# Four PSUM banks for the transposes of an attention kernel, and pauses that hold DMA issues back

## The chip, the cores and the metric

The kernel runs on one core of one Trainium2 chip. The metric is the device time of one execution in microseconds (us). The engines have these names in the profile: PE is the matmul engine (PEld its weight loads), DVE the vector engine, ACT the scalar engine, POOL the general engine, and SP the engine that here only issues DMAs (SPq is its queue).

## The reference

Attention over q, k, v of shape 4 batches x 8 heads x 576 rows x 64, with a threshold, then a Fourier mixing with an MLP, then a gated convolution:

```python
scores = q @ k.T / sqrt(64)
attn = exp(where(scores >= max(scores) - tau, scores, -1e9) - max(scores))
x = (attn / (sum(attn) + 1e-9)) @ v                  # heads side by side: 4 x 576 x 512
u = x + real(fft(fft(x, axis=seq), axis=features))
un = (u - mean(u)) / sqrt(var(u) + 1e-6)
y = u + relu(un @ w_ch1) @ w_ch2                     # 512 -> 2048 -> 512
out = (sigmoid(causal_conv5(y)) * (y @ w_val)) @ w_out
```

## The kernel before, in words

**Tiles.** Two heads make a pair, so there are 16 pairs, four for each batch. A pair has 9 tiles of 128 score rows by 576 keys: four of its first head, four of its second, and one that holds the last 64 rows of both. `g_tile(g)` describes the life of tile g (0 to 143), one step per `yield`:

- PE makes the scores `s` (L641) in one of two double banks of PSUM;
- DVE takes the negated row maximum `neg` (L706), ACT the exponential `e` (L712), DVE the thresholded product `p` with its row sum `su` (L723). After `p` the double bank of `s` is free for the scores of the tile after next;
- the reciprocal of `su` is taken for two tiles at once (L656, L658), and POOL scales `p` by it (L731);
- PE transposes `p` in four blocks into one bank `t` (L739), and ACT copies the bank to `m` (L756).

`g_tail` transposes the last 64 columns of each row tile (L668, L672), `g_pv` multiplies by v (L421) in ten matmuls for each part of a pair, `g_fold` and `g_mirror` fold the output with its mirror image by way of DRAM, and `g_fft` makes the Fourier transform of a batch (L540 and L553). The MLP's first chunk is `g_h` (L1201) and `g_c` (L1237), the mean for its variance is a matmul at L1113, and its other four chunks are L1047 and L1063.

**PSUM.** There are eight banks: four for `s`, two in `ps_t` for `t`, and two in `ps_f`, named `f`, for all other results (tails, v product, Fourier transform, means). Both pools are used in turn, so a new tile waits for the release of the one before the last of its own pool.

**What sets the order.** The kernel is written out by a planner at build time, `Loom`. Each generator asks for an engine, a cost in ns and a rank, or for a condition: `"after"` (marks of other generators), `"when"` (a test), `"delay"` (a time). `Loom.step` always takes the request that can start first by its own clock, and the code that follows the `yield` then emits the instructions. Each engine later runs what was emitted for it in exactly that order. So a rule or a cost of the planner changes the order of all five engines, and no instruction's own work. A request with `"room"` needs a bank of `ps_f`: `Loom.start` holds it until the tile before the last was freed.

Before the change, `"delay"` only moves the time from which the next engine request may start:

```python
elif kind == "delay":
    t.ready += args[0]
```

When the generator goes on with something that is not an engine request, such as a DMA on SP, the pause has no effect: the DMA is emitted at once. Three pauses are of that kind: the one ahead of `g_mirror` (L457 to L459), which reads back from DRAM (L440) what L453 has just stored there; 4000 ns ahead of the return of a conversion buffer (L916); and 200 ns ahead of the weight loads of `g_give`. Where a condition follows (`"when"` in `g_convert`), it is tested at once and buffers are taken at once, and only the engine request behind it keeps the pause.

**Weights.** The MLP's weights come as 64-bit numbers and are converted in pieces (`g_convert`: DVE L251, L252, L255 to L257, ACT L253, L254, POOL L261). The first pieces are stored to DRAM (`e_h`, `e_l`, SP L912) and loaded back (SP L872) once the attention's buffers are free; later ones are converted in place. Six `raw` and `cv` buffers carry this work.

Of the kernel before, what the change touches and what calls it, by code (L numbers as in the profile page):

```python
# [11 lines left out]
F32 = mybir.dt.float32  # L12
# [64 lines left out]
class Loom:  # L77
# [33 lines left out]
    def settle(self, t):  # L111
        while t.want is not None:
            kind, *args = t.want
            if kind == "after" and all(k in self.done for k in args):
                t.ready = max([t.ready] + [self.done[k] for k in args])
            elif kind == "delay":
                t.ready += args[0]
            elif kind == "when" and args[0]():
                t.ready = max(t.ready, self.clock)
            else:  # L120
                return
            t.want = next(t.gen, None)
            if t.want is None:
                self.tasks.remove(t)
# [16 lines left out]
    def start(self, t):  # L141
        e, ns, rank, *how = t.want
        s = max(self.now[e], t.ready)
        room = next((x for x in how if x.startswith("room")), None)
        if room:
            k = room, self.put.get(room, 0) - 2
            if k[1] >= 0:
                if k not in self.done:
                    return None
                s = max(s, self.done[k])  # L150
        return s

    def cost(self, t, s):
# [27 lines left out]

    def step(self, until=None):
        picks = [x for x in (self.pick(e) for e in self.now) if x]
        if not picks:
            return False
        s, t = min(picks, key=lambda x: x[0])
        if until is not None and s > until:
            return False
        e, ns, rank, *how = t.want
        ns = self.cost(t, s)  # L190
        if e == "PE":
            self.shape, self.last = how[0], t
        if "port" in how:
            self.port[e] = s + ns - 50.0
        self.now[e] = s + ns - self.OVER[e]
        self.clock = s
        self.end = s + ns + self.SIGNAL[e]
        t.ready = self.end
        self.pull(t)
        self.wake()  # L200
        return True
# [88 lines left out]
def attention_fft(tc, right, ps_f, a, u_d, dram, conv_w, loom):  # L290
    nc = tc.nc
    PE, DVE, ACT, POOL, SP = nc.tensor, nc.vector, nc.scalar, nc.gpsimd, nc.sync
    right1 = ExitStack()
    with ExitStack() as right2, ExitStack() as right2b, ExitStack() as right3, ExitStack() as right4, ExitStack() as scores, ExitStack() as turned:
        def pool(stack, name, bufs, side="right", **kw):
            return stack.enter_context(tc.tile_pool(name=name, bufs=bufs, side=side, **kw))
# [13 lines left out]
        ps_t = pool(turned, "ps_t", 2, space=PSUM)  # L310
# [73 lines left out]
        def fill_tile():  # L384
            return ps_f.tile([128, 512], F32, tag="f", name="f"), loom.room()
# [9 lines left out]
        def pt_tile(p, c):  # L395
            if (p, c) not in pt:
                pt[p, c] = (pt0_p, pt1_p)[c].tile([128, 2, 4, 256] if c == 0 else [128, 4, 640], F32, tag=f"m{c}", name=f"m{c}")
            return pt[p, c]

        def g_pv(p, c):  # L400
# [29 lines left out]
            if c == 1:  # L430
                loom.add(g_fold(p))
# [3 lines left out]
        def g_mirror(b):  # L435
            if b:
                yield "after", ("spent", b - 1)
            for i in range(2):
                m = mirror[b, i] = fft_p.tile([128, S], F32, tag=f"mirror{i}", name="mirror")
                SP.dma_start(out=m, in_=rev_d[b][i * 128:(i + 1) * 128])  # L440
            loom.mark("mirror", b, after=8000.0)

        def g_fold(p):
            b, j = p // NP, PAIRS[p % NP]
            yield "after", ("x", p, 0), ("x", p, 1), *([("folded", p - 1)] if p else [])
            x = xt.pop(p)
# [4 lines left out]
            if j >= 2:  # L451
                r = 1 + 128 * (3 - j)
                SP.dma_start(out=rev[r:r + 128], in_=x)  # L453
                if j == 2:
                    SP.dma_start(out=rev[0:1], in_=x[127:128])
                loom.mark("folded", p)
                if p % NP == 1:  # L457
                    yield "delay", 6000.0
                    loom.add(g_mirror(b))  # L459
                return  # L460
            SP.dma_start(out=xs[j * 128:(j + 1) * 128], in_=x)
# [5 lines left out]
            t = [tmp_p.tile([128, KE], F32, tag="xf", name="xf") for _ in range(2)]  # L467
# [214 lines left out]
        def g_tile(g):  # L682
            p, h, i = tiles[g]
            u, j = divmod(g, 2)
            c = 0 if i < 2 else 1
# [27 lines left out]
            if h != 1:  # L713
                n = p * 5 + i - PBUFS
                if n >= 0:
                    yield "after", ("tailed", *divmod(n, 5))
                    q, r = divmod(n, 5)
# [12 lines left out]
            v = p_view(g)  # L730
            POOL.tensor_scalar(out=v, in0=v, scalar1=ssum[u][:, j:j + 1], scalar2=1.0, op0=ALU.mult, op1=ALU.mult)  # L731
            loom.mark("n", g)
            yield "after", *([("t", g - 1)] if g else [("n", 0)]), *([("mc", g - 2)] if g > 1 else []), *([("pv", p - 2, c)] if p > 1 else [])
            yield "PE", 437.0, 0.5, "full"
            m = pt_tile(p, c)
            f = ps_t.tile([128, 4, 128], F32, tag="t", name="t")
            pv = v[:, TAIL if h == 1 else 0:]
            for t in range(4):
                PE.matmul(out=f[:, t, :], lhsT=pv[:, t * 128:(t + 1) * 128], rhs=ident, is_transpose=True, start=(t == 0), stop=(t == 3))  # L739
# [13 lines left out]
            else:  # L753
                x = h * 320 + (i - 2) * 128
                o, fv = m[:, :, x:x + 128], f
            ACT.activation(o, fv, AF.Copy)  # L756
            loom.mark("mc", g)

        idle = e_p.tile([128, 2, HALF], F32, tag="e", name="idle")[:, 0, 0:128]
        DVE.memset(idle, 0.0)  # L760
        f = ps_t.tile([128, 4, 128], F32, tag="t", name="idle")
# [20 lines left out]
        loom.end = 8500.0  # L782
        loom.mark("kq", 0)
        loom.add(g_tile(0))

        def g_late():
# [834 lines left out]
```

## Time and profile before

| | |
|---|---|
| median of 3 runs | 874.63 us (873.76 to 875.32) |
| the profiled execution | 873.72 us |
| its span, first to last instruction | 871.9 us |
| around the span | 1.82 us |
| busy share: PE, DVE, ACT, POOL | 95%, 64%, 48%, 44% |
| mean granted PE clock | 0.992 of full speed |

The attention takes the first 340 us, with the Fourier transform and the first weight conversions between its tiles. The MLP and the gate fill the rest. The profile gives, for each engine, its busy time, its idle time, and for an idle stretch the instruction that ended it (its releaser). A wait is put down to the engine whose signal came last.

### The profile page before, as it was taken

The page shows a single profiled execution, that of the slowest core. Times are in us where ns is not written, and L with a number is a line of the kernel's source. Part 1 is how long each engine was busy: PE and PEld are TensorE (multiplying, and loading weights), DVE is VectorE, ACT ScalarE, POOL GpSimd, SP SyncE. Part 2 cuts the span into 40 slices and gives each one's busy share as a digit, 9 for nine tenths or more (in the row PEclk, how much of TensorE's full clock was granted, in tenths as well). Part 3 has the DMA queues.
Part 4 walks back from the last instruction along what each step waited for, and adds up shares of the span by engine and source line. Part 5 has one row for each costly group of instructions (what it writes and reads, how often), then busy time and mean ns, then how long its engine had stood idle before and what let it go on. Part 6 is the DMA issues. An engine that isn't in the chain of part 4 may idle for free.

```text
span 871.9 us, 13881 instructions
## 1 busy us (share of the span) xinstructions
PE 830.0 (95%) x4886; PEld 653.7 (75%) x4886; DVE 556.8 (64%) x1212; ACT 421.0 (48%) x855; POOL 386.3 (44%) x450
## 2 busy tenths in 40 slices
PE   6999989989999997999999999999999999999998
PEld 4555556656656655788889999987888788898996
DVE  6999898888889985879846742223213646428740
ACT  3878777777758754664535332141123131134431
POOL 3466874597678564666443431013010210076421
PEclk9999999999999999999999999999999999999999
DMA  7369465536654338989316523004000320432111
GB/s 209 79 197 236 120 151 152 166 114 207 202 172 124 123 111 284 349 285 337 126 50 239 169 81 90 1 1 133 1 1 0 103 103 0 166 143 91 61 49 61
DMA packets 62733, 115.27 MB, mean 132 GB/s; under 512 B 14530, under 2 KB 21698, under 8 KB 62664
## 3 DMA queue, kind: packets, MB, share of 16 engines
q1 hardware_dynamic: 55128, 90.53, 32.5%
q0 software_dynamic: 7104, 23.57, 8.9%
q8 instruction: 39, 0.64, 0.3%
q10 hardware_dynamic: 432, 0.30, 0.2%
q14 instruction: 30, 0.25, 0.1%
HBM read 82.90 MB, written 31.47 MB: 131 GB/s over the span
## 4 chain that ended last, share of the span: by engine, by line
PE 65%; DVE 12%; issue 9%; ACT 6%; POOL 4%; DMA 3%; SPq 0%; DVEq 0%; ACTq 0%; POOLq 0%
PE c L1063 14%; PE h L1047 14%; PE f L421 6%; PE s L641 6%; PE v L1434 5%; PE o L1452 5%; PE c L1237 4%; PE h L1201 4%; PE t L739 4%; DVE neg L706 4%; DVE p L723 3%; ACT e L712 2%; POOL p L731 2%; ACT m L756 2%; PE f L540 1%
## 5 line engine op out<-in xcount | busy, mean ns | idle before, releaser
L731 POOL TENSOR_SCALAR p<-p,su 128x576 f32<-128x576 f32 x144 | 111.8, 786 | 96.7 <-DVE su L658 78.5
L1051 DVE SCALAR_TENSOR_TENSOR hl<-h,hh 128x384 fp32r<-128x384 f32 (+1 forms) x64 | 39.9, 624 | 150.4 <-ACT hh L1050 146.7
L1050 ACT ACTIVATE hh<-h 128x384 fp32r<-128x384 f32 (+1 forms) x64 | 34.8, 544 | 208.4 <-PE h L1047 202.3
L712 ACT ACTIVATE e<-s,neg 128x576 f32<-128x576 f32 x144 | 104.8, 742 | 55.2 <-DVE neg L706 41.5
L723 DVE SCALAR_TENSOR_TENSOR p<-s,thr,e 128x576 f32<-128x576 f32 x144 | 114.3, 816 | 12.9 <-ACT e L712 4.1
L641 PE MATMUL s<-kt,qt 64*128 64x288 f32 (+1 forms) x640 | 102.2, 453 | 13.5 <-DVE p L723 9.5
L706 DVE TENSOR_REDUCE neg<-s 128x1 f32<-128x576 f32 x144 | 103.9, 749 | 17.4 <-PE s L641 16.6
L739 PE MATMUL t<-ident,p 128*128 128x128 f32 x576 | 90.3, 286 | 13.6 <-ACT m L756 7.2
L739 PEld LDWEIGHTS t<-ident,p 128*128 128x128 f32 x576 | 63.7, 143 | 44.7 <-POOL p L731 23.1
L1063 PE MATMUL c<-hl,w1h 128*128 128x384 f32 (+1 forms) x256 | 92.8, 363 | 0.5 <-DVE hl L1051 0.5
L1063 PE MATMUL c<-hh,w1h 128*128 128x384 f32 (+1 forms) x256 | 92.6, 362 | 0.0
L1063 PE MATMUL c<-hh,w1l 128*128 128x384 f32 (+1 forms) x256 | 92.6, 362 | 0.0
L641 PEld LDWEIGHTS s<-kt,qt 64*128 64x128 f32 (+1 forms) x640 | 47.5, 181 | 54.6 <-issue 25.6
L756 ACT ACTIVATE m<-t 128x512 f32<-128x512 f32 x144 | 83.2, 599 | 4.8 <-PE t L739 4.2
L421 PE MATMUL f<-m,v 128*64 128x320 f32 (+1 forms) x512 | 72.5, 421 | 0.0
L1047 PE MATMUL h<-unh,w0h 128*128 128x384 f32 (+1 forms) x256 | 62.6, 364 | 1.2 <-ACT unh L1028 1.1
L1047 PE MATMUL h<-unl,w0h 128*128 128x384 f32 (+1 forms) x256 | 62.4, 363 | 0.3
L1047 PE MATMUL h<-unh,w0l 128*128 128x384 f32 (+1 forms) x256 | 61.6, 362 | 0.0
L421 PEld LDWEIGHTS f<-m,v 128*64 128x64 f32 x512 | 34.4, 140 | 28.1 <-issue 9.2
L1072 POOL TENSOR_TENSOR res<-ht,res 128x512 f32<-128x512 f32 (+1 forms) x20 | 23.0, 1185 | 68.7 <-DVE ht L1071 68.7
L1063 PEld LDWEIGHTS c<-hl,w1h 128*128 128x128 f32 x256 | 48.1, 188 | 6.3 <-DVE hl L1051 1.3
L1047 PEld LDWEIGHTS h<-unh,w0h 128*128 128x128 f32 x256 | 46.7, 188 | 7.5 <-ACT unh L1028 2.5
(259 smaller groups left out, 1662.9 us busy)
## 6 DMA issues: line engine op xcount, KB each, us to landing
raw<-in_moe_w_ch POOLq DMA_DIRECT2D x32, 512.0 KB, 5.6
qt<-in_q SPq DMA_DIRECT2D x30, 288.0 KB, 5.1
kt<-in_k SPq DMA_DIRECT2D x15, 432.0 KB, 3.9
ypad<-y_d SPq DMA_DIRECT2D x16, 288.0 KB, 4.1
out<-os SPq DMA_DIRECT2D x18, 256.0 KB, 2.0
v<-in_v SPq DMA_DIRECT2D x16, 256.0 KB, 2.7
e_h<-cx SPq DMA_DIRECT2D x16, 256.0 KB, 3.7
e_l<-ct SPq DMA_DIRECT2D x16, 256.0 KB, 2.3
```

What stands on the lines that cost most here:

```text
L421: PE.matmul(out=f[h * 64:h * 64 + 64, 0:n], lhsT=w, rhs=r, start=(t == 0), stop=(t == 4))
L641: PE.matmul(out=s[o, c, 0:HALF], lhsT=qt[w, hh, q], rhs=kt[w, 2 if h == 2 and hh else hh], start=True, stop=True)
L706: DVE.tensor_reduce(out=neg[u][:, j, 0:1], in_=sc[g][:, :, 0:HALF], axis=AX.XY, op=ALU.max, negate=True)
L712: ACT.activation(e, sc[g][:, :, 0:HALF], AF.Exp, bias=neg[u][:, j, 0:1], scale=1.0)
L723: DVE.scalar_tensor_tensor(out=p_view(g).rearrange("p (a b) -> p a b", a=2), in0=sc.pop(g)[:, :, 0:HALF], scalar=thr[u][:, j:j + 1], in1=e ...
L731: POOL.tensor_scalar(out=v, in0=v, scalar1=ssum[u][:, j:j + 1], scalar2=1.0, op0=ALU.mult, op1=ALU.mult)
L739: PE.matmul(out=f[:, t, :], lhsT=pv[:, t * 128:(t + 1) * 128], rhs=ident, is_transpose=True, start=(t == 0), stop=(t == 3))
L756: ACT.activation(o, fv, AF.Copy)
L1047: PE.matmul(out=f[:, 0:n], lhsT=ww[:, k * 128:(k + 1) * 128], rhs=x[:, k, 0:n], start=(i == 0), stop=(i == 3 * KB - 1))
L1063: PE.matmul(out=ch[c][o][:, 0:n], lhsT=ww[:, o * 128:(o + 1) * 128], rhs=x, start=(at_ == 0 and i == 0), stop=(at_ == FB - 1 and i == 2))
L1434: PE.matmul(out=f[:, 0:HALF], lhsT=w[:, k, o * 128:(o + 1) * 128], rhs=x[:, k, s], start=(i == 0), stop=(i == 3 * KB - 1))
L1452: PE.matmul(out=f, lhsT=x[:, k, d], rhs=w[:, k], start=(i == 0), stop=(i == 3 * KB - 1))
```

## The change

Three things change, all in the planner and its requests.

1. `"delay"` becomes a request of its own, `"until"`, that the planner's clock must reach before the generator goes on. Whatever follows, a DMA issue or the return of a buffer too, is emitted only then.
2. The transpose asks for `"room_t"` or `"room"`: the planner looks at the bank of `ps_t` and the bank of `ps_f` that would be next, and takes `ps_t` if it is free by then, else the one that is free first. The wait for mark `("mc", g - 2)`, the copy of the tile before the last, is gone; the copy now frees the bank that the tile took.
3. The pause ahead of the mirror's load is 8000 ns in place of 6000.

```diff
             elif kind == "delay":
-                t.ready += args[0]
+                t.want = "until", max(t.ready, self.clock) + args[0]
+                continue
+            elif kind == "until" and self.clock >= args[0]:
+                t.ready = max(t.ready, args[0])
...
-        room = next((x for x in how if x.startswith("room")), None)
-        if room:
-            k = room, self.put.get(room, 0) - 2
-            if k[1] >= 0:
-                if k not in self.done:
-                    return None
-                s = max(s, self.done[k])
+        rooms = [(x, self.put.get(x, 0) - 2) for x in how if x.startswith("room")]
+        if rooms:
+            free = [(self.done[k] if k[1] >= 0 else 0.0, k[0]) for k in rooms if k[1] < 0 or k in self.done]
+            if not free:
+                return None
+            when = min(free)[0]
+            t.place = next(x for w, x in free if w <= max(s, when))
+            s = max(s, when)
...
                 if p % NP == 1:
-                    yield "delay", 6000.0
+                    yield "delay", 8000.0
                     loom.add(g_mirror(b))
...
-            yield "after", *([("t", g - 1)] if g else [("n", 0)]), *([("mc", g - 2)] if g > 1 else []), *([("pv", p - 2, c)] if p > 1 else [])
-            yield "PE", 437.0, 0.5, "full"
+            yield "after", *([("t", g - 1)] if g else [("n", 0)]), *([("pv", p - 2, c)] if p > 1 else [])
+            yield "PE", 437.0, 0.5, "full", "room_t", "room"
             m = pt_tile(p, c)
-            f = ps_t.tile([128, 4, 128], F32, tag="t", name="t")
+            if loom.place == "room":
+                f, room = fill_tile()
+                f = f.rearrange("k (t q) -> k t q", t=4)
+            else:
+                f, room = ps_t.tile([128, 4, 128], F32, tag="t", name="t"), loom.room("room_t")
...
             ACT.activation(o, fv, AF.Copy)
+            loom.free(room)
             loom.mark("mc", g)
```

`step` also gains the lines that move the clock on to the next pause's end when no engine request starts before it.

The lines of the changed file are numbered higher: 641 becomes 651, 739 becomes 753, 421 becomes 431, 553 becomes 563, 1201 becomes 1216, 440 becomes 450, 872 becomes 887, 912 becomes 927. The order of the instructions changes on every engine. 132 of the 144 transposes still go to `ps_t`, 12 to `ps_f`. Three places follow.

PE in the middle of the attention, before: two score tiles (x4: two matmuls for each, four for the last tile of a pair; the trace shows each of them as two records), then the transposes of three tiles in one go (x12: four blocks each).

```order
L421 MATMUL f<-th_320_200,vt_196 64x320 x2
L641 MATMUL s<-kt,qt 128x288 x4
L739 MATMUL t<-ident,p 128x128 x12
L672 MATMUL f<-ident,p 64x64 x2
L641 MATMUL s<-kt,qt 128x288 x4
L739 MATMUL t<-ident,p 128x128 x4
```

The same piece of the program in the changed kernel (the end of the same v product, 64x320, stands in it).

```order
L651 MATMUL s<-kt,qt 128x288 x4
L431 MATMUL f<-m_1026,v_195 64x320 x2
L431 MATMUL f<-th_320_200,vt_196 64x320 x2
L753 MATMUL t<-ident,p 128x128 x8
L651 MATMUL s<-kt,qt 128x288 x4
L682 MATMUL f<-ident,p 64x64 x2
L431 MATMUL f<-m_1167,v_193 64x256 x6
L753 MATMUL t<-ident,p 128x128 x8
```

Two transposes at a time, and other work of PE behind them. Rows of x12 stand in the order before at five places, and at none in the changed order.

PE between the last score tiles and the MLP's first matmul, before: nine transposes follow the last scores, the last six of them here, with stage-2 matmuls of the third batch (L553) between; then the MLP's `h`, with the three last v products still to come behind it.

```order
L553 MATMUL f<-csl,aeh 128x290 x2
L739 MATMUL t<-ident,p 128x128 x4
L553 MATMUL f<-csl,aeh 128x290
L668 MATMUL f<-ident,p 128x128 x2
L739 MATMUL t<-ident,p 128x128 x8
L553 MATMUL f<-ssh,boh 128x290 x3
L739 MATMUL t<-ident,p 128x128 x8
L668 MATMUL f<-ident,p 128x128 x2
L739 MATMUL t<-ident,p 128x128 x4
L553 MATMUL f<-ssh,bol 128x290 x3
L553 MATMUL f<-ssl,boh 128x290 x3
L1201 MATMUL h<-unh,w0h_4203 128x512 x4
```

The same place now: six transposes follow the last scores, the last two of them here, and the tail and all three v products stand ahead of `h`.

```order
L563 MATMUL f<-ssl,boh 128x290 x2
L753 MATMUL t<-ident,p 128x128 x4
L678 MATMUL f<-ident,p 128x128 x2
L753 MATMUL t<-ident,p 128x128 x4
L682 MATMUL f<-ident,p 64x64 x2
L431 MATMUL f<-m_3898,v_193 64x320 x8
L431 MATMUL f<-th_320_198,vt_194 64x320 x2
L431 MATMUL f<-m_4099,v_195 64x256 x8
L431 MATMUL f<-th_256_199,vt_196 64x256 x2
L431 MATMUL f<-m_4228,v_195 64x320 x8
L431 MATMUL f<-th_320_200,vt_196 64x320 x2
L1216 MATMUL h<-unh,w0h_4202 128x512 x4
```

Two thirds of `h` 0 stood ahead of the v products before, none of it now. Between the v products and the variance's mean matmul (L1113) the order before has the rest of `h` 0, `h` 1, `c` 0, `h` 2 and three quarters of `c` 1 (the number is that of a block of 128 hidden units); the changed order has `h` 0, a third of `h` 1, 18 stage-2 matmuls of the third batch, `c` 0 and the rest of `h` 1. The fourth batch's first stage (L540) follows directly now; before, the rest of `c` 1 and a third of `h` 3 stood between. In DVE's queue the reciprocal for the last two tiles has two conversion instructions (L251, L252) ahead of it behind the last `p`, where there was one (L251).

SP's queue before the first load of converted weights, before: the mirror's load directly behind the store that it reads (xr_3861), and two stores of converted weights.

```order
L453 DMA xr_3861<-xt 128x576
L440 DMA mirror<-xr_3861 128x576 x2
L912 DMA e_h<-cx 128x512
L912 DMA e_l<-ct 128x512
L872 DMA w0h_4203<-e_h 128x512
```

The same place now: four stores of converted weights stand between the store (xr_3827) and its mirror's load.

```order
L463 DMA xr_3827<-xt 128x576
L927 DMA e_h<-cx 128x512
L927 DMA e_l<-ct 128x512
L927 DMA e_h<-cx 128x512
L927 DMA e_l<-ct 128x512
L450 DMA mirror<-xr_3827 128x576 x2
L887 DMA w0h_4202<-e_h 128x512
```

## Rows read from the trace of the kernel before

**Rows 1.** The page: the span, and the engines' busy time.
```profile
span 871.9 us, 13881 instructions
...
PE 830.0 (95%) x4886; PEld 653.7 (75%) x4886; DVE 556.8 (64%) x1212; ACT 421.0 (48%) x855; POOL 386.3 (44%) x450
```

**Rows 2.** Windows: length, busy time by engine (PE, PEld, DVE, ACT, POOL), clock, DMA.
```profile
20.00:326.00 306.00, 285.16 (x2089) 179.41 (x2093) 272.12 (x659) 226.43 (x492) 206.87 (x262) 0.98 0.53 153
340.00:450.00 110.00, 108.25 (x535) 86.93 (x534) 80.85 (x129) 56.03 (x106) 58.09 (x66) 0.99 0.71 244
450.00:760.00 310.00, 307.97 (x1529) 275.60 (x1529) 132.00 (x241) 84.75 (x148) 60.42 (x55) 1.00 0.23 76
```

**Rows 3.** Waits of PE: total us, times, longest.
```profile
PE s L641 <- DVE p L723: 9.5, 15, 2.1
PE t L739 <- ACT m L756: 7.2, 16, 0.8
PE t L739 <- POOL p L731: 5.4, 11, 0.8
PE h L1201 <- DMA w0h<-e_h: 4.3, 1, 4.3
```

**Rows 4.** Timeline of PE, 176 to 196 us: start, length, instructions, idle before.
```profile
178.27 1.09 PE L739 MATMUL t<-ident,p 128*128 128x128 f32 x8
180.10 0.63 PE L739 MATMUL t<-ident,p 128*128 128x128 f32 x4 [0.74 <-ACT m L756]
180.66 0.76 PE L641 MATMUL s<-kt,qt 64*128 64x288 f32 x4
...
189.00 1.24 PE L641 MATMUL s<-kt,qt 64*128 64x288 f32 x8
```

**Rows 5.** Timeline of PE, 296 to 350 us.
```profile
314.89 2.44 PE L641 MATMUL s<-kt,qt 64*128 64x288 f32 x8 [1.45 <-DVE p L723]
...
326.39 0.66 PE L739 MATMUL t<-ident,p 128*128 128x128 f32 x4
326.80 0.38 PE L553 MATMUL f<-csh,aeh 97*128 97x290 f32 x1
```

**Rows 6.** The chain that ended last: a stretch of stage-2 matmuls.
```profile
308.19 3.08 PE f L553 x23
```

**Rows 7.** Timeline of PE, 338 to 400 us.
```profile
338.75 1.82 PE L1201 MATMUL h<-unh,w0h 128*128 128x512 f32 x4 [4.27 <-DMA w0h<-e_h]
...
342.21 0.45 PE L672 MATMUL f<-ident,p 128*64 128x64 f32 x4
...
350.13 1.19 PE L1201 MATMUL h<-unl,w0h 128*128 128x512 f32 x4
...
353.89 0.39 PE L1237 MATMUL c<-hh,w1h 128*128 128x512 f32 x1
...
356.61 1.07 PE L1201 MATMUL h<-unh,w0h 128*128 128x512 f32 x4
...
362.66 0.50 PE L1113 MATMUL mean<-cs,ones 128*128 128x512 f32 x1 [0.89 <-DVE cs L1162]
...
364.62 0.40 PE L540 MATMUL f<-cdh,xeh 128*97 128x258 f32 x2
```

**Rows 8.** SP's queue: its waits at L440, and the first weight load's issue.
```profile
SPq L440 <- DMA xr<-xt: 11.9, 4, 5.3
...
334.04 0.49 SPq L872 DMA_DIRECT2D w0h<-e_h  x1
```

**Rows 9.** Timeline of POOL: the last two scalings of p, the fold's last step.
```profile
330.05 1.57 POOL L731 TENSOR_SCALAR p<-p,su 128x576 f32<-128x576 f32 x2 [3.73 <-DVE su L658]
...
361.37 0.70 POOL L485 TENSOR_TENSOR xel<-xf,xeh 128x289 fp32r<-128x289 f32 x1 [0.56 <-ACT xeh L483]
```

**Rows 10.** Windows around two long waits of PE; the clock is behind POOL's time.
```profile
314.00:320.00 6.00, 5.09 (x28) 2.59 (x30) 5.17 (x15) 2.69 (x6) 4.05 (x6) 0.72 0.55 180
338.00:344.00 6.00, 5.25 (x24) 3.40 (x26) 2.58 (x3) 0.22 (x1) 3.48 (x4) 0.72 1.00 356
```

More of the change, by code (lines that the diff above doesn't have):

```diff
@@ L183, in step @@
         picks = [x for x in (self.pick(e) for e in self.now) if x]
-        if not picks:
-            return False
-        s, t = min(picks, key=lambda x: x[0])
-        if until is not None and s > until:
-            return False
+        rests = [t.want[1] for t in self.tasks if t.want[0] == "until"]
+        if not picks and not rests:
+            return False
+        s, t = min(picks, key=lambda x: x[0]) if picks else (None, None)
+        if until is not None and min(rests + [s] if picks else rests) > until:
+            return False
+        if rests and (not picks or min(rests) <= s):
+            self.clock = max(self.clock, min(rests))
+            self.wake()
+            return True
         e, ns, rank, *how = t.want
@@ L195, in step @@
         self.now[e] = s + ns - self.OVER[e]
-        self.clock = s
+        self.clock = max(self.clock, s)
         self.end = s + ns + self.SIGNAL[e]
         t.ready = self.end
+        self.place = getattr(t, "place", None)
         self.pull(t)
```

## The prediction

> **What bounds the kernel now.** I read the page first: PE is busy for 830.0 of 871.9 us [rows 1], so the question is where its 42 idle us lie. The windows by stage answer it. From 20 to 326 us, the attention, PE works 285.2 of 306 us and DVE 272.1, so two engines are close to full and PE idles 20.8 us; from 340 to 450 us PE idles 1.8 us, and from 450 to 760 us 2.0 [rows 2]. The MLP is PE's own work and the change touches none of it. What the change can win is idle time of PE ahead of 340 us, and every us won there moves the whole rest.
>
> The list of PE's waits says what that idle time is: 9.5 us for DVE to free a score bank, 7.2 us in 16 waits for ACT to empty a transpose bank, 5.4 us for POOL's scaled p, and one wait of 4.3 us for the first weight of the MLP [rows 3]. The timeline shows a bank wait: transposes of two tiles from 178.27, and the third only at 180.10, 0.74 us idle, because ACT has not copied the first out [rows 4]. It also shows the long wait: PE stands at h until 338.75 for w0h, whose load SP issued at 334.04 [rows 7, 8]. SP was late because it stood at the mirror's loads (11.9 us over the four of them, 5.3 us in the longest) for the store that they read back [rows 8].
>
> A long wait costs twice. In the 6 us around 338.75 the granted clock is 0.72, and likewise around the wait of 1.45 us that ended at 314.89 [rows 5, 10]: part of it at 1.2 GHz, after PE had been idle. A mean of 0.72 over 6 us means 3.4 us at half speed, so about 1.7 us of PE's work lost each time.
>
> **The change part by part.** The profiled execution is the base: 871.9 us of span and 1.82 around it, 873.72; the median of the runs is 0.9 above it.
>
> *Bank waits.* Priced by the trace's steps (0.41 us for a tile's transposes, from 326.39 to 326.80 [rows 5]; 1.24 for two score tiles [rows 4]; 0.13 for a stage-2 matmul, 3.08 over 23 [rows 6]; 7.9 for a tail and three v products, 342.21 to 350.13 [rows 7]), the order says how much work PE has between the end of a tile's transposes and the next use of that bank. Before, it is under 1.0 us at 24 tiles, and what is missing to 1.0 us sums to 7.4 us, which is the 7.2 us of the trace [rows 3]. After, it is under 1.0 us at 8 tiles and 1.3 us are missing. So some 5.9 us of bank waits go, although only 12 tiles take a bank of the other pool: the gain is in the order around them. It pays in full only where PE, not DVE, sets the pace at that spot. Lower bound: nothing, if each saved wait returns as a wait for DVE, which has 33.9 us of idle time in 306 [rows 2]. Upper bound: 5.9. PE has less slack than DVE (20.8 against 33.9), so I take two thirds, **-4.0**.
>
> *The MLP's start.* The wait of 4.3 us and its 1.7 us of slow clock go: the three v products, 7.9 us, now stand ahead of h, so PE comes to h later than w0h lands. From the last scores (their successor starts at 326.39 [rows 5]) w0h took 12.4 us even with SP held up; PE now needs about 13.5 (4.45 to the last but one transpose, below, two tiles and tails 1.1, v products 7.9). The SP hold-up itself is shortened too, since four other stores stand between store and mirror; nothing waits for that any more, so it is worth nothing beyond this. That is -6.0. Three things give some of it back.
> First, between the last scores and the last two transposes PE has now four tiles (1.6 us), nine stage-2 matmuls (1.2) and a tail (0.3): 3.1 us. But the last two p leave POOL one after the other in 1.57 us from 330.05, so the first of them at 330.84 [rows 9], 4.45 us after the scores. PE waits 1.3 us, plus up to 0.4 for one more conversion step ahead of the reciprocal on DVE. Behind this transpose stand the v products and the whole MLP. I take +1.4.
> Second, the mean of the variance: PE waited 0.89 us for its second half, which began at 362.66 [rows 7], so it had come there at 361.8, 11.6 us after the v products ended at 350.13. Now it has 24 h matmuls to do on that way (5.4 us; 16 of them took 3.76, from 350.13 to 353.89), 18 of stage 2 (2.4), one c (2.7, from 353.89 to 356.61) [rows 7] and the first half (0.4): 10.9. So it arrives 0.7 earlier at a chain of DVE and ACT that has two more steps in front. +0.7 to +1.6; I take +1.1.
> Third, the first stage of the last batch started at 364.62, 14.5 us after the v products [rows 7]; its fold ended on POOL at 362.07, 11.9 us after them [rows 9]. Now PE comes there 10.9 us after them plus its wait at the mean, about 12. No wait by this sum, but no room either; 0.
> Together **-3.5**, between -6.0 and 0.
>
> *More changes of shape.* PE goes from one matmul shape to another (scores on 64 rows, v products on 64 columns, the rest full) 170 times before its first h in the old order and 177 in the new. A score tile alone takes 0.76 us, two in one go 1.24 [rows 4], so a split costs at most 0.28: 7 of them 2.0, and nothing where a pipeline hides it. I take **+1.0**.
>
> *Fuller fill banks.* Up to the first h the two f banks carry 124 tiles instead of 110. Spaced as above, 10 of them come within 1.0 us of their bank's last use, 2 before; what is missing to 1.0 us is 2.1 us against 0.7. PE's list has no wait of this kind now, so between 0 and +1.4: **+0.7**.
>
> *The held pauses.* They keep conversion buffers 4 us longer and SP freer. The order has one more weight piece converted before the last p than before, and is ahead or level at every h of the first chunk, so DVE's conversion work is not late for the MLP, where PE idles 1.8 us in 110 [rows 2]. The waits for DVE, 9.5 us [rows 3], should stay about as they are: counted in the same way, the new order has no more tight spots between score pairs than the old, and one of them, near tile 60, is as tight as the one that cost 1.45 us at 314.89 [rows 5]. **0**, and 1.7 either way for a slow stretch more or less.
>
> **Sum.** -4.0 - 3.5 + 1.0 + 0.7 = -5.8: 867.9 against 873.72, and 868.8 against the median. I forecast **869 us**.
>
> **Rivals.**
> *DVE takes it all.* The scores go in pairs and have two double banks, so a pair cannot start before DVE has done with the one before. If that lockstep sets the pace everywhere, the bank term is 0 and the sum is -1.8: 872.8. For it: PE waits longer for DVE than for banks [rows 3]. Against it: DVE idles 33.9 us in the same stretch.
> The Trainium skill, TensorE: Matmul & The Clock Gate, section HAM oscillation, speaks for this rival: it reports a kernel that double-buffered PSUM and gained nothing further (126.6 to 125.5 us). By that rule the bank term would be 0 here; the 16 waits of the list speak against it.
> *All of it pays.* Bank waits 5.9, the start 6.0 with the returns hidden, no cost for shapes and banks: -11.9, 862.7.
> *Slower: the fold comes late.* PE, in order, now stands at the last batch's first stage about 2.5 us earlier behind the v products than before, and its chain runs over DVE, POOL and ACT. Each us that the fold ends later than 12 us after the v products is a us of the end, and a long wait adds 1.7 us of slow clock. If PE waits there for 4.1 us, the gain of 5.8 is gone; from 5.9 us of wait the kernel is slower by 0.2%, and 8 us give 868.8 + 8 + 1.7 = 878.5. For it: POOL and DVE queues are reordered there, and POOL's steps are slow (0.70 to 1.4 us). Against it: the fold's first DVE step stands one place earlier in DVE's queue now.
>
> **How the numbers follow.** My forecast (faster, 862.5 to 873) has 0.62, all of it paying 0.08, DVE taking it 0.15, slower 0.15. A run of this kernel can tell 0.2%, 1.75 us, from no change: faster 0.70, same 0.15, slower 0.15. The range 862 to 877 leaves out the ends of the second and the last case; the likeliest case alone is 863 to 873.
>
> **What would show it.** Right: PE's waits for ACT at L739 (now L753) down from 7.2 to 1 or 2 us; no wait for w0h and no slow clock there; a new wait of 1 to 2 us for POOL's p just ahead of the tail; waits for DVE near 9.5 us. Wrong: waits of PE for DVE grown by what the bank waits lost; a wait of several us at L540 or at the mean in the first 30 us of the MLP; new stretches at half clock in the attention.

## The result, and the profile after

The changed kernel takes **862.72 us** (median of 4 runs, 861.90 to 866.56), the kernel before 874.19 on the same chip: a ratio of 0.9884, 95% interval 0.9854 to 0.9914, so 1.2% faster. The forecast was 869, in a range of 862 to 877: sign and range hold, and the gain is twice the one forecast. The time is also that of the rival "all of it pays" (862.7), but by another sum, as shown below. The profiled execution has a span of 860.5 us, 11.4 less than before [rows 1]. The page's span and busy time:

```profile
span 860.5 us, 13891 instructions
...
PE 825.1 (96%) x4886; PEld 651.8 (76%) x4886; DVE 553.5 (64%) x1212; ACT 421.3 (49%) x855; POOL 388.1 (45%) x450
```

Of the 11.4 us, PE's busy time gives 4.9 and its idle time 6.5. The list of PE's waits, as in [rows 3]:

```profile
PE s L651 <- DVE p L733: 6.8, 11, 2.1
PE t L753 <- POOL p L741: 6.1, 12, 1.0
PE f L550 <- POOL xel L495: 2.8, 1, 2.8
...
PE t L753 <- ACT m L770: 1.8, 5, 0.5
...
PE f L753 <- POOL p L741: 0.9, 2, 0.7
...
PE f L550 <- ACT th L688: 0.8, 2, 0.5
```

The waits for ACT at the transposes fell from 7.2 to 1.8 us, those for DVE from 9.5 to 6.8, and that for w0h is gone. Those for POOL's p grew from 5.4 to 7.0 (t and f together). New are a wait of 2.8 us for the fold (xel) and short ones for fill banks that ACT has not emptied yet (f behind th). The windows of the attention and of the first 110 us of the MLP, as in [rows 2]; they end earlier, so the bounds are moved:

```profile
20.00:320.00 300.00, 283.26 (x2097) 177.93 (x2096) 271.81 (x661) 228.29 (x494) 206.07 (x259) 1.00 0.55 162
330.00:440.00 110.00, 107.23 (x534) 89.04 (x531) 79.39 (x128) 54.83 (x104) 62.89 (x70) 1.00 0.66 232
```

Up to the last scores PE idles 16.7 us where it idled 20.8. The clock is 1.00 throughout; before, stretches at half clock near 251, 317 and 341 us cost 1.7 us each (the last two are in [rows 10]), together 5.1 us of busy time, so that the rest of the busy time is level, +0.2. (Ahead of 26 us matmuls take their long durations in both.) PE's timeline, with the places of [rows 5, 7]:

```profile
259.74 1.09 PE L753 MATMUL t<-ident,p 128*128 128x128 f32 x8
261.49 1.38 PE L753 MATMUL f<-ident,p 128*128 128x128 f32 x8 [0.66 <-POOL p L741]
...
319.85 0.65 PE L753 MATMUL t<-ident,p 128*128 128x128 f32 x4
...
324.71 0.66 PE L753 MATMUL t<-ident,p 128*128 128x128 f32 x4 [0.86 <-POOL p L741]
...
334.02 1.20 PE L1216 MATMUL h<-unh,w0h 128*128 128x512 f32 x4
...
344.80 0.72 PE L1128 MATMUL mean<-cs,ones 128*128 128x512 f32 x2
...
348.65 0.36 PE L550 MATMUL f<-cdh,xel 128*97 128x258 f32 x1 [2.77 <-POOL xel L495]
```

The work behind the last scores starts at 319.85 (before 326.39), `h` at 334.02 without a wait, the mean at 344.80 without one (before 362.66, with 0.89). The MLP's second chunk starts at 438.89 (before 450.50). So 6.5 us are won up to the last scores, 5.1 from there to the second chunk, and 0.2 of it is lost after. SP's queue around the mirror, as in [rows 8]:

```profile
316.46 0.91 SPq L450 DMA_DIRECT2D mirror<-xr  x2
317.42 0.67 SPq L887 DMA_DIRECT2D w0h<-e_h  x1
...
339.06 0.61 SPq L620 DMA_DIRECT2D xd<-xs  x1
```

w0h is asked for at 317.42, before the last scores end, where it was 334.04. POOL's queue at the fold, the counterpart of [rows 9]:

```profile
346.40 0.90 POOL L595 TENSOR_TENSOR xd<-xd,dd 128x289 f32<-128x289 f32 x1 [2.83 <-DVE hl L1230]
347.26 0.69 POOL L597 TENSOR_TENSOR xd<-xd,sm 128x287 f32<-128x287 f32 x1
347.90 0.69 POOL L495 TENSOR_TENSOR xel<-xf,xeh 128x289 fp32r<-128x289 f32 x1
```

The fold's last step (xel) stands in POOL's queue behind two additions to xd, the third batch's result, and the first of them waits 2.83 us. The releaser named (hl) is no input of it: what DVE makes for it (dd, sm) was done at 341.79. But xd itself is a load from DRAM. The list of DMA issues from 336 to 349 us (KB, us to landing):

```profile
xd<-xs SPq DMA_DIRECT2D x1, 288.0 KB, 7.2
```

339.06 and 7.2 make 346.3, and POOL goes on at 346.40; the trace's semaphore events agree, POOL's wait for this load ends at 346.27. So a load that shares its 7 us with loads of the MLP's weights holds the addition, the addition holds xel, and xel makes PE wait 2.8 us. The other input of xel, xeh, was ready at 344.58 (ACT), before PE came there.

### The profile page after: what moved, and what is told of

It is laid out like the page before. It is cut to its first block, busy times and chain, and to the rows that moved or that the text cites. A ratio compares the mean times of both kernels' runs of the same rounds, so it can differ in the third digit from the quotient of the medians.

```text
span 860.5 us, 13891 instructions
## 1 busy us (share of the span) xinstructions
PE 825.1 (96%) x4886; PEld 651.8 (76%) x4886; DVE 553.5 (64%) x1212; ACT 421.3 (49%) x855; POOL 388.1 (45%) x450
## 4 chain that ended last, share of the span: by engine, by line
PE 65%; DVE 13%; issue 9%; POOL 6%; ACT 4%; DMA 1%; SPq 0%; DVEq 0%; ACTq 0%; POOLq 0%
PE c L1078 14%; PE h L1062 14%; PE v L1449 5%; PE o L1467 5%; PE s L651 5%; PE h L1216 5%; PE c L1252 5%; DVE neg L716 5%; PE f L431 4%; DVE p L733 4%; POOL p L741 4%; PE t L753 3%; ACT e L722 2%; PE f L563 2%; PE f L550 1%
## 5 line engine op out<-in xcount | busy, mean ns | idle before, releaser
L741 POOL TENSOR_SCALAR p<-p,su 128x576 f32<-128x576 f32 x144 | 111.0, 780 | 93.1 <-DVE su L668 81.5
L651 PE MATMUL s<-kt,qt 64*128 64x288 f32 (+1 forms) x640 | 100.3, 450 | 10.8 <-DVE p L733 6.8
L753 PE MATMUL t<-ident,p 128*128 128x128 f32 x528 | 82.7, 285 | 10.0 <-POOL p L741 6.1
L753 PEld LDWEIGHTS t<-ident,p 128*128 128x128 f32 x528 | 58.3, 143 | 41.3 <-POOL p L741 27.2
L770 ACT ACTIVATE m<-t 128x512 f32<-128x512 f32 x132 | 76.2, 600 | 10.4 <-PE t L753 9.4
```

Of the source, the lines that this page charges most:

```text
L651: PE.matmul(out=s[o, c, 0:HALF], lhsT=qt[w, hh, q], rhs=kt[w, 2 if h == 2 and hh else hh], start=True, stop=True)
```

## The experiments

**How the runs are compared.** The planner writes another order for any change of a cost, so most of these edits move work all over the attention. To compare the runs I cut each profile at two places: at the last scores and at the first matmul of the second chunk.

- *Attention* is the time at which the last scores end, plus the work that the order leaves PE between there and the second chunk, at full speed, less what the slow clock lost between 26 us and the last scores. The work is counted in each kernel's order and priced: stage 2 at 0.135 us, first stage 0.12, a tile's transposes 0.41, four `h` or `c` matmuls 0.906, a v product with 320 columns 2.86, with 256 columns 2.38, and 3.5 for tails, means and the rest, nearly the same in every order.
- *Start* is what the stretch up to the second chunk takes beyond that work: waits and slow clock.

For before: 326.46 + 115.9 - 3.4 = 439.0, and 450.50 - 326.46 - 115.9 = 8.1. Before, e3 and e10 have one order up to the last scores, and so have the changed kernel and e8: the attention of one order differs by up to 1.1 us between executions. The expectations of e11 and e12 quote a count up to 0.6 us different, and that of e11 leaves the slow clock in (442.4 for before). In the table "own two" means the two banks of `ps_t` alone, "four" those of `ps_f` too. The diffs of e3 and e10 are against the kernel before, the others against the changed kernel. A *tight* transpose, in the expectations, is one that comes less than 1.0 us of PE's work behind the last use of its bank, as counted in the prediction.

| kernel | rule for banks | pauses | median us | attention | start |
|---|---|---|---|---|---|
| before | own two | old | 873.7 to 874.9 | 439.0 | 8.1 |
| e3, before, `h` behind | own two | old | 872.99 | 438.7 | 7.3 |
| e10, before, mirror later | own two | one held | 869.01 | 439.8 | 4.8 |
| e2, hold only | own two | held | 867.32 | 439.4 | 4.0 |
| e5, before at 441 | own two | old | 872.62 | 438.2 | 10.2 |
| e6, before at 433 | own two | old | 871.98 | 439.5 | 7.3 |
| changed kernel | four | held | 862.72 | 435.7 | 3.2 |
| e8, first stage later | four | held | 864.53 | 436.0 | 6.7 |
| e1, bank only | four | old | 861.87 | 435.9 | 1.6 |
| e4, changed at 441 | four | held | 864.91 | 433.4 | 7.6 |
| e7, changed at 433 | four | held | 875.21 | 436.0 | 14.1 |
| e11, bank only at 441 | four | old | 866.05 | 440.7 | 2.3 |
| e12, bank only at 433 | four | old | 867.49 | 436.9 | 9.0 |
| e9, changed, own banks | four planned, two used | held | 872.76 | 443.8 | 3.2 |

My theory (A): two sources that add up, the bank rule in the attention and the wait for w0h at the start.

**e1, the bank choice alone.**

```diff
-                t.want = "until", max(t.ready, self.clock) + args[0]
-                continue
+                t.ready += args[0]
...
-                    yield "delay", 8000.0
+                    yield "delay", 6000.0
```

> Kernel before with the choice of banks alone; pauses and the mirror's 6000 ns as before. In its order 7 transposes come less than 1.0 us of PE work after the last use of their bank, 1.4 us missing (before: 24 and 7.4), and h 0 stands ahead of the three v products again. Theory A, the gain has two sources that add up, bank waits in the attention and the wait for w0h: PE's waits of a transpose for ACT near 1.5 us, the last scores some 6 us earlier than before's 326.4, the wait for w0h still there with 3 to 6 us, so about 868 us. Rival B, the pauses bring it all by freeing SP and DVE: within 1 us of before, 874. Rival C, any new order moves the time by several us, whatever the edit: no sum of parts, anything from 863 to 876.

Measured: 861.87 us, ratio 0.984 (0.9816 to 0.9864): all of the gain, and below every range given. PE's waits:

```profile
PE s L650 <- DVE p L732: 9.1, 11, 2.2
PE t L752 <- POOL p L740: 8.2, 14, 1.0
PE t L752 <- ACT m L769: 2.1, 6, 0.5
PE f L752 <- POOL p L740: 1.8, 3, 0.9
```

The bank waits went as expected, but PE waits 10.0 us for POOL's p, where it was 5.4: most of what the banks saved is waited for again one step on. No wait for w0h stands in the list, against what A said: in this order SP issues the mirror's load at 311.33 and w0h's at 313.12, 11.5 us ahead of `h`. B is out: the held pauses are not needed.

**e2, the held pauses alone** (the transposes' old rule put back).

```diff
...
-            yield "PE", 437.0, 0.5, "full", "room_t", "room"
+            yield "PE", 437.0, 0.5, "full"
...
```

> Changed kernel with the old rule for the transpose (bank of ps_t only, behind the copy of the tile before the last); the held pauses and the mirror's 8000 ns stay. In its order 18 transposes are tight, 6.3 us missing (before 24 and 7.4), a third of h 0 stands ahead of two of the three v products. Theory A: PE's waits of a transpose for ACT 5.5 to 6.5 us, waits for DVE near 9.5, the wait for w0h shorter than 4.3 by what SP is freed, 0 to 2 us: 867 to 871. Rival B, the pauses bring it all: 863 to 865, with waits for DVE down by 2 to 3 us as in the changed kernel. Rival C: anything from 863 to 876.

Measured: 867.32 us, ratio 0.9906 (0.9883 to 0.9929).

```profile
PE s L651 <- DVE p L733: 8.3, 13, 2.2
...
PE t L749 <- ACT m L766: 5.4, 14, 0.7
```

The bank waits stay, as A said. But its gain of 7.5 us and the 13 of e1 sum to far more than the 11.5 of both: the parts do not add up, and A falls as it was put. The start gains 4 us here, with SP freed, and 6.5 in e1 without that.

**e3, `h` behind the v products, in the kernel before.**

```diff
-            yield "after", ("split", 0), ("placed", ids[j, 0]), *([("h", j - 1)] if j else [])
+            yield "after", ("split", 0), ("placed", ids[j, 0]), ("h", j - 1) if j else ("pv", 15, 1)
```

> Kernel before with one added condition: h 0 may only start behind the last v product. Nothing else moves ahead of it; 24 tight transposes and 7.4 us missing stay. Theory A, the start of the MLP is worth what its wait and slow clock cost: no wait for w0h, the stretch from the last scores to the second chunk 4 to 6 us shorter, 868 to 870. Rival, the wait goes on to the next in line, the mean or the last batch's fold: a wait of several us at L1113 or L540 and 873 to 875.

Measured: 872.99 us, ratio 0.9983 (0.9962 to 1.0004). The wait for w0h is gone and the start is only 0.8 us better. PE's timeline in its first stage 2 of the last batch:

```profile
370.76 0.57 PE L553 MATMUL f<-csl,aeh 97*128 97x290 f32 x3
372.88 1.09 PE L553 MATMUL f<-ssh,boh 96*128 96x290 f32 x3 [1.55 <-ACT ny L566]
373.77 0.93 PE L553 MATMUL f<-ssh,bol 96*128 96x290 f32 x3
```

A new wait of 1.55 us, and then three matmuls take 0.93 in place of 0.57: stage 2 runs at half clock to 379.6, which loses 3.4 us. With 0.75 for `sm` ahead of the v products and 0.5 at the fold, 6.2 us are lost again of the 6.0 and 0.9 (at the mean) that the edit had won. The rival was right, though the place is another one than it named.

**e10, the last mirror's load held, nothing else.** The order on PE, DVE, ACT and POOL stays word for word. The planner's code behind `"until"` is that of the changed kernel, and only this one pause uses it.

```diff
...
+            elif kind == "hold":
+                t.want = "until", max(t.ready, self.clock) + args[0]
+                continue
...
-                    yield "delay", 6000.0
+                    yield ("hold" if b == B - 1 else "delay"), 6000.0
```

> Kernel before with the pause ahead of the last batch's mirror held, and nothing else: the order on TensorE, DVE, ACT and POOL stays word for word, SP alone puts two stores and the four loads of the first weights ahead of the mirror's load. This prices the MLP's wait for w0h by itself. If SP's place behind the mirror is its cause: the wait of 4.3 us shrinks to under 2, and 1.7 us of slow clock go with it: 868 to 870. The mirror's load comes some 3 us later; if the fold and the mean behind it are late by that, a wait of 2 to 4 us at L1113 or L540 takes it back: 873 to 875.

Measured: 869.01 us, ratio 0.9929 (0.9901 to 0.9956). SP's queue, and PE's timeline:

```profile
325.94 1.39 SPq L884 DMA_DIRECT2D w0h<-e_h  x1
...
329.76 0.79 SPq L452 DMA_DIRECT2D mirror<-xr  x2
```

```profile
313.58 0.76 PE L653 MATMUL s<-kt,qt 64*128 64x288 f32 x4 [1.45 <-DVE p L735]
...
331.81 1.08 PE L1213 MATMUL h<-unh,w0h 128*128 128x512 f32 x4
...
396.10 0.44 PE L1125 MATMUL mean<-cs,ones 128*128 128x384 f32 x1 [1.23 <-DVE cs L1115]
```

Counted from the last scores, w0h is issued 5.6 us earlier than in [rows 8], and the mirror's load no later (5.8 us behind them in both). `h` starts without a wait or slow clock. The cause of that wait is shown: SP's place behind the mirror. The start gains 3.3 of the 6.0 us; 0.4 comes back at w0l, 1.2 at the second chunk's mean, and 1.1 I can't place.

This run shows something else. Its 1.45 us wait at 313.58 is that of [rows 5], in the same order, but the clock behind it is full, 1.00 where [rows 10] have 0.72:

```profile
314.00:320.00 6.00, 5.65 (x46) 3.11 (x44) 5.66 (x13) 2.86 (x7) 4.74 (x7) 1.00 0.44 139
```

In e3, in that order too, it is 0.72 again. So the 3.4 us of slow clock in the attention of the kernel before are not fixed by the order: two executions of it have them (before, e3), one has not.

**e4 to e7, orders shuffled for no reason:** the planner's cost of a transpose at 441 or 433 ns, under the new rule (e4, e7) and the old one (e5, e6). The edit of e4:

```diff
-            yield "PE", 437.0, 0.5, "full", "room_t", "room"
+            yield "PE", 441.0, 0.5, "full", "room_t", "room"
```

> Changed kernel with the planner's cost of a transpose at 441 ns in place of 437, so that its order is shuffled and the rules stay: 9 tight transposes, 2.3 us missing, 22 of 144 in the other pool; here h 0 comes ahead of the v products again and behind 25 more Fourier matmuls. Theory A, the rule brings the gain: waits for ACT 1.5 to 3 us and 863 to 866. Rival C, one order among many: outside of 862 to 867, up to 874.

Measured: 864.91 us, ratio 0.9878 (0.9853 to 0.9903). The time was A's, but its waits for ACT were not (1.5 to 3 us expected). And with these waits it has the shortest attention of all, 433.4:

```profile
PE t L753 <- ACT m L770: 6.7, 13, 0.8
```

> Kernel before, old rules throughout, with the planner's cost of a transpose at 441 ns in place of 437: an order shuffled for no reason, 13 tight transposes and 4.6 us missing by chance (before: 24 and 7.4), a third of h 0 ahead of the v products. After the four runs above the theory of two separate sources is in doubt, since each half of the change brought more than its part. Theory A, the rules matter: 872 to 876. Theory D, the order of before happened to carry about 9 us of accidents (wait for w0h 4.3 and 1.7 of slow clock, two slow stretches in the attention of 1.7 us each) that almost any other order is free of, and only the bank waits belong to the rule: 865 to 868, no wait for w0h over 1 us, no slow stretch near 250 and 315 us, waits for ACT of 4 to 6 us.

Measured: 872.62 us, ratio 0.9984 (0.996 to 1.0009). D, the bad luck of one order, fails: the attention has no slow stretch and the waits for ACT are 5.0 us, as D said, but the time is A's, and this order has a w0h wait of its own. Its timeline:

```profile
353.80 1.55 PE L1201 MATMUL h<-unh,w0h 128*128 128x512 f32 x4 [2.15 <-DMA w0h<-e_h]
```

> The same with 433 ns: 19 tight transposes, 6.7 us missing. Theory A: 872 to 876. Theory D: 865 to 869, waits for ACT of 5.5 to 7 us, no wait for w0h over 1 us.

Measured: 871.98 us, ratio 0.9966 (0.9948 to 0.9985). No w0h wait over 0.2 us, but waits of 1.6 at the mean and 1.3 in the first stage. D fails here too.

> Changed kernel with 433 ns: 7 tight transposes, 1.3 us missing, a third of h 0 ahead of the last two v products. Theory A and D alike: the bank waits stay at 1 to 3 us, and the kernel within 861 to 865, some 4 us under the two orders with the old rule. If the new rule brings nothing of its own, it lies among them, 865 to 868.

Measured: 875.21 us, ratio 1.0 (0.9978 to 1.0023). That is outside every range given. Its attention is as good as the changed kernel's (436.0), and the start loses 14.1 us. PE's waits in that stretch, from 317 to 452 us:

```profile
PE c L1252 <- ACT hh L1228: 3.4, 5, 0.7
PE h L1216 <- DMA w0h<-e_h: 1.4, 1, 1.4
PE h L1216 <- POOL w0l L271: 1.4, 2, 1.1
```

Weights come late from loads and from conversion, and `hh` and `hl` from ACT and DVE, with all of the change in place. All waits of that stretch sum to 9.0 us and its slow stretch lost 1.7; of the other 3.4 a part lies right behind the waits for `hh`, where `c` matmuls start 0.33 to 0.39 us apart, at full clock, that otherwise start 0.23 apart.

**e8, the last batch's first stage later**, to take away the changed kernel's wait of 2.8 us.

```diff
+            if b == B - 1:
+                yield "delay", 3000.0
```

> Changed kernel, with the last batch's first Fourier stage held back by 3000 ns in the planner: the order up to the mean is the same word for word on TensorE, then 12 c and 4 h matmuls, 3.6 us, stand ahead of the first stage. If the wait of 2.8 us for xel is a cost of the changed kernel, it goes and nothing takes its place: 860 us, 2.8 less. If the chain behind it (parts, stage 2, the adds, the second chunk's norm) is what counts later, the wait turns up there, at stage 2 or the second chunk's first h: 862.5.

Measured: 864.53 us, ratio 0.9863 (0.9832 to 0.9894), no gain over 862.72 and 2 us over the rival's 862.5. The wait at the fold is gone and turned up at another place than the two that the rival named:

```profile
361.02 0.50 PE L1254 MATMUL c<-hl,w1h 128*128 128x512 f32 x1 [2.20 <-DVE hl L1232]
...
362.97 0.63 PE L1254 MATMUL c<-hh,w1h 128*128 128x512 f32 x1
```

2.2 us, and now with half clock behind it (0.63 for a matmul that takes 0.40), 1.7 us lost.

**e9, the changed kernel's order with the old banks.**

```diff
...
-                f, room = fill_tile()
-                f = f.rearrange("k (t q) -> k t q", t=4)
+                f, room = ps_t.tile([128, 4, 128], F32, tag="t", name="t"), loom.room("room")
...
```

> Changed kernel, in exactly its order on all engines, but the 12 transposes that the planner gave a bank of ps_f take the next bank of ps_t after all. Counted as in the prediction, 22 transposes are then tight and 7.1 us missing (changed kernel 8 and 1.3; before 24 and 7.4). If the order around them is what saves the bank waits, as the prediction put it: waits for ACT at 2 to 3 us and 863. If the 12 banks themselves do, the 7.1 us are waited for again: PE's waits for ACT 6 to 8 us, the attention 4 to 6 us longer, 867 to 869.

Measured: 872.76 us, ratio 0.9979 (0.9962 to 0.9996): 12 tiles' banks are worth 10 us in this order by the medians, 8.1 by the two profiles, more than the 4 to 6 expected. PE's waits and timeline, and ACT's timeline:

```profile
PE t L752 <- ACT m L769: 10.2, 12, 2.1
```

```profile
264.27 1.09 PE L752 MATMUL t<-ident,p 128*128 128x128 f32 x8
267.44 1.12 PE L752 MATMUL t<-ident,p 128*128 128x128 f32 x8 [2.08 <-ACT m L769]
```

```profile
265.41 1.41 ACT L722 ACTIVATE e<-s,neg 128x576 f32<-128x576 f32 x2 [1.28 <-DVE neg L716]
266.71 1.08 ACT L769 ACTIVATE m<-t 128x512 f32<-128x512 f32 x2
```

This is the place of 261.49 in the changed kernel, where the second two transposes went to f banks after 0.66 us, for p. Here they wait for the copies, which ACT's queue has behind two exponentials, and these for DVE. The attention is 8.1 us longer, and the waits for ACT grew by 8.4.

**e11 and e12, two more orders under the new rule** (e1 with 441 and 433 ns).

> Choice of banks alone, old pauses, transposes costed at 441 ns: one more order under the new rule, 6 tight and 1.7 us missing. The runs so far, read as the time of the last scores plus the full-speed work left from there to the second chunk, put the attention of the five orders with the old rule at 438.3 to 442.4 us and of the five with the new one at 433.5 to 436.1; what the stretch from the last scores to the second chunk takes beyond its work was 2.1 to 14.0 us with no tie to a rule. So this one: attention 433 to 437, start anywhere from 2 to 10, 861 to 869 us in all. If the rule's gain in the attention is luck, 438 to 442.

Measured: 866.05 us, ratio 0.9902 (0.9875 to 0.993). Attention 440.7, longer than in any of the old rule's four orders, and in the range named for luck. Two of its waits:

```profile
239.38 0.63 PE L752 MATMUL t<-ident,p 128*128 128x128 f32 x4 [1.52 <-ACT m L769]
...
318.30 0.66 PE L752 MATMUL t<-ident,p 128*128 128x128 f32 x4 [1.66 <-POOL p L740]
```

4.9 us of waits for ACT where the count of tight places had 1.7.

> Choice of banks alone with transposes costed at 433 ns: a fifth independent order under the new rule, 7 tight and 1.8 us missing. Last scores plus the full-speed work left behind them, less slow clock, was 438.3 to 439.8 us in the old rule's orders, 433.5 to 436.1 in four of the new rule's and 440.8 in the one before this. If the rule's gain in the attention holds as a rule, with that one an exception: 433 to 437 here, waits for ACT 1.5 to 3 us. If the count of tight transposes tells nothing of an order's waits: 438 or more. The start takes 2 to 10 us beyond its work in either case, so 861 to 871 in all.

Measured: 867.49 us, ratio 0.9916 (0.9894 to 0.9938). Attention 436.9, as the rule would have it; waits for ACT 3.1; start 9.0, for the most part by the fold. PE's timeline, and POOL's:

```profile
355.37 0.53 PE L549 MATMUL f<-cdh,xel 128*97 128x258 f32 x1 [5.15 <-POOL xel L494]
```

```profile
352.36 1.29 POOL L594 TENSOR_TENSOR xd<-xd,dd 128x289 f32<-128x289 f32 x1 [4.92 <-DVE cs L1190]
```

It is the changed kernel's fold wait grown to 5.15 us, again by the addition to xd ahead of xel: SP issued xd's load at 342.76, and it took 9.5 us. PE's next 5.5 us are at half clock. The prediction's rival "the fold comes late" exists; it struck another order of the same rule.

## Why the prediction was right, and where its sizes were off

The direction and both mechanisms were right for this order: the waits for ACT are 1.8 us (1 to 2 forecast), the wait for w0h and its slow clock are gone. PE waits 0.9 us for p just ahead of the tail (1 to 2 forecast). What was off are sizes. Up to the second chunk 11.6 us were won where 5.8 were summed; of the difference 3.4 is slow clock in the attention, 1.4 the start, and 1.0 the rest of the attention. So the time of "all of it pays" was met by luck: that rival had 5.9 and 6.0 and no slow clock, and measured are 3.3, 4.9 and 3.4. Two of the prediction's own signs failed: the waits for DVE are 6.8 us and not near 9.5, and the wait of 2.8 us at the first stage is of the kind that was listed as a sign of being wrong.

*Slow clock, 0 with 1.7 either way.* This is the term that was off by most. The two stretches of half clock in the attention of the kernel before, 1.7 us each, are absent from the changed kernel's profile: 3.4 of the 11.4. e10 shows that the same waits in the same order can go without them, so no run shows that the change took them away. The mean clock of the changed kernel's four executions is 0.999 (the profiled one), 0.995, 0.991 and 0.997, and the one at 0.991 is the fastest, 861.90 us. So a mean clock doesn't tell where the slow clock fell or what it cost.

*Bank waits, -4.0 of 5.9.* 5.4 us of waits for ACT went, near what the count had, and did not come back as waits for score banks. But they did not come out as idle time saved in full. From 20 us to the last scores PE idles 4.1 us less, although the waits for ACT fell there by 5.2 and those for DVE by 2.7: waits for fill banks behind th (1.8), for p (0.7) and others grew. So two thirds was near the mark, but the reason given for it, DVE's slack, was not what took the rest.

The other reason I gave, "the gain is in the order around them", is refuted by e9: in that order the 12 banks are everything, and without them the waits are 10.2 us. The planner packs transposes closer because it has a bank for them.

*What the rule is worth in any order.* Four orders under the old rule have attentions of 438.2 to 439.5 us (before, e2, e5, e6), six under the new one 433.4 to 440.7 (changed, e1, e4, e7, e11, e12; e3, e8 and e10 repeat an order). The means are 439.0 and 436.4, a difference of 2.6; this order gained 3.3, and my net term for the attention, -4.0 + 1.0 + 0.7 = -2.3, was near that. Not all of the 2.6 is shown to be waits. From 26 us to the last scores PE idles 18.2 to 20.8 us in the four orders (mean 19.5) and 16.3 to 21.9 in the six (mean 18.3): the waits for ACT fall in the mean from 5.3 to 3.4 us, those for p grow from 5.9 to 6.9. The other 1.4 is busy time for the same matmuls, of which e1 and e4 have less for a reason that I can't give. So some 1 to 3 us belong to the rule, with e11 as an order that gains nothing. e4 and e11 also show that the count of tight places, which fitted before (7.4 against 7.2) and after (1.3 against 1.8), is no safe measure of another order: 6.7 and 4.9 us waited where it had 2.3 and 1.7.

*Waits for DVE, 0.* They fell by 2.7. e1 and e2 have 9.1 and 8.3, so neither part does that by itself; it is this order's.

*Shapes +1.0, fill banks +0.7.* Attention without slow clock gained 3.3 while idle time up to the last scores fell by 4.1 (20.8 to 16.7): 0.8 went elsewhere. That is near the +1.0 for shapes, but no run shows that it is shapes. The waits behind th, 1.8 us, are more than the upper end of 1.4 for fill banks.

*The MLP's start, -3.5.* Measured -4.9 (8.1 to 3.2). By terms: the wait and its slow clock, -6.0, as forecast; p, +0.9 for +1.4; the mean, -0.9 for +1.1, since its chain was done when PE came there 10.8 us behind the v products (10.9 forecast, where 5.4 for the 24 h matmuls should be 5.6 by the prediction's own rows); the fold, +2.8 for 0. The 12 us from the v products to the fold became 14.5, because xel stands in POOL's queue behind an addition that waits for a load; I had looked at the fold's first step in DVE's queue and not at what stands ahead of its last one in POOL's. With 0.7 less for hh that sums to -3.9; 1.0 stays unplaced.

And this term is no gain of a rule at all. The start takes 1.6 to 14.1 us beyond its work: old pauses 1.6 to 10.2, held ones 3.2 to 14.1. e5 and e7 have waits for w0h again. e10 shows what the hold-up of SP costs where it strikes; whether it strikes hangs on the order. *The rival "DVE takes it all"* fails as it was put: the waits for score banks grew in none of the six orders (4.6 to 9.1 us, 9.5 before). A relative of it is alive: in e1 the bank waits saved came back as waits for p, and on the changed kernel's page POOL, ahead of its scalings of p, stands idle 93.1 us, 81.5 of them until DVE's su. The Trainium skill, TensorE: Matmul & The Clock Gate, section HAM oscillation, had a kernel to which PSUM double-buffering gave no further gain. Here, in one order, PE waits 10.2 us for ACT with two banks and 1.8 with four (e9 and the changed kernel), so that result does not carry over to this kernel.

e1, at 861.87, is not told apart from the changed kernel: the intervals 0.9816 to 0.9864 and 0.9854 to 0.9914 meet. So the choice of banks alone would have been enough, with the order that it got; no version beat both clearly.

## What to carry to other kernels

A rule of a planner can't be priced from one order. Shuffle the order for no reason under the old rule and the new one, cut the profiles into stages, and compare stage by stage: here one rule's six orders spread over 861.9 to 875.2 us, more than the change brought, while the stage that the rule concerns spread by 3.5 us in five of them and the sixth was 3.8 beyond. A wait that is moved away from an in-order engine is worth its length only if what stands next in line is ready; look at the queue of each of its inputs up to the last step, loads included.

## What was not expected of the hardware

In the 14 profiles there are 30 waits of PE of 1.2 us or more between 26 and 460 us. With 10 of them goes a stretch at half clock, behind the wait or, in e12, begun within it, and 20 have none. The stretches lost 1.7 us of work each, or 2.8 and 3.4 (e12, e3). Length alone doesn't decide: 5.15 (e12) and 2.2 us (e8) had one, 2.77 (changed kernel) and 2.6 (e9) none, and a 1.38 us wait near 126.5 us had one in e6 and none in before and e5. Two short waits in a row, 1.09 and 0.35 us near 249, had one in before and e3 and none in e10. That a long wait "costs twice" was true of two of the three in the profile that the prediction read, and of a third of all.
